# Gate logits from kept transposes: two product blocks a batch instead of four

## The chip, the cores and the metric

The kernel runs on one core of one Trainium2 chip. The metric is the device time of a run in microseconds (us), lower is better. Beside the times of plain runs there is one profiled execution, from which all rows of the trace come.

## The reference

Causal attention over 8 batches, 8 heads, 576 positions and head size 64, with a decay bias from cumulative sums of `s`. Its output, as 4608 tokens of 512 values, goes through a mixture of 8 experts: logits are `x @ w_gate`, tokens are assigned greedily by falling logit with at most 576 tokens an expert, and each expert is a two-layer ReLU network.

```python
scores = scale * np.matmul(q, k.transpose(0, 1, 3, 2))
scores = np.where(causal, -1e9, scores + np.minimum(bias, 0.0))
attn = softmax(scores)                 # maximum taken off, sum + 1e-9
x = np.matmul(attn, v)                 # as N = 4608 tokens x D = 512
logits = x @ w_gate                    # w_gate: 512 x 8
order = np.argsort(-logits.flatten())  # greedy: token and expert once each, 576 tokens an expert
out[mask_e] = np.maximum(x[mask_e] @ w1[e], 0.0) @ w2[e]
```

The change is in the line of the logits.

## The kernel before

**Two parts.** Attention runs first, for 16 groups `g` (a batch `b` = g // 2 and a half `hf` = g % 2 of its heads), each with two passes `pr` of two heads `par`. The experts follow, with a router that picks each expert's tokens.

**Numbers in two pieces.** A value is kept as a hi piece in f16 and a lo piece that holds what f16 left out; a product of two such values takes three matmuls: hi by hi, hi by lo, lo by hi.

**A pass of attention.** `spass` (lines 431 to 501) takes scores on TensorE (PE) into `pss` (three PSUM banks), and VectorE (DVE) takes the row maxima from them at line 442. `sts` (503 to 559) takes the transposed scores into `pst` (three banks, lines 514, 515, 517); ScalarE (ACT) takes exp of them at 525, and GpSimd (POOL) forms the lo piece `R` at 527. `pv` (561 to 592) multiplies with V into `po` (two banks, columns 0 to 324). `norm` (594 to 609) divides by the sums on DVE (lines 602, 603, 604), writes the hi piece of x on ACT (606) and the lo piece on DVE (608) into `xp`. When a batch is done, `xout` stores `xp` into `xs` in DRAM from the SP queue (616, 618).

**The logits.** A pass fills 128 of the 512 columns of x for the 576 tokens of its batch: a quarter `c` = 2 hf + pr. `turn` (621 to 658) transposes that quarter, hi and lo, five token tiles each, on PE (635) into a bank of `pss`, copies it with ACT (638) into `xt` (a ring of three), and multiplies it with the gate `wgp` (645). These products go into columns 340 to 499 of one of the two `po` banks, chosen by the parity of the batch, with one sum for each quarter, token tile and expert. After quarter 3, DVE adds the four quarters (651) into the logits `L`. The router's first steps (lines 797 to 809) run on DVE for batches 0 to 3, 4 to 6 and 7. The expert part begins with `ge` (line 886).

**Order.** Every instruction is a task of `Plan`, a list scheduler with an engine, a duration that the code states, a priority and the buffers that it uses. It plays the schedule through with these stated durations and writes each engine's queue in that order; at run time each queue is served in order. A `Ring` gives out buffers; a ring of one gives the buffer again only when all tasks that use it stand in the plan. The bank of the products isn't among their `uses`. Semaphores are put in by the framework.

Of the kernel before, what the change touches and what calls it, by code (L numbers as in the profile page):

```python
# [10 lines left out]
F16 = mybir.dt.float16  # L11
BF = mybir.dt.bfloat16
I32 = mybir.dt.int32
AF = mybir.ActivationFunctionType
OP = mybir.AluOpType
AX = mybir.AxisListType
# [7 lines left out]
E = 8  # L24
# [180 lines left out]
class Attention:  # L205
# [11 lines left out]
    def rings(self):  # L217
        w, ps = self.w, self.ps
        R = lambda pool, shape, dt, name, n, o=True: Ring([pool.tile(shape, dt, name=f"{name}{i}") for i in range(n)], o)
        self.r = dict(  # L220
            raw=R(w, [128, 2, 2, S], F32, "raw", 2), rv=R(w, [128, 2, 9, D], F32, "rv", 2),
            QK=R(w, [128, 2, 2, 2, HB], F16, "QK", 4),
            V=R(w, [128, 2, 9, 65], F16, "V", 3), Vl=R(w, [128, 2, 9, 64], F16, "Vl", 3),
            P=R(w, [128, 2 * PW + 192], F32, "P", 2), R=R(w, [128, 2 * PW + 192], F16, "R", 2),
            mr=R(w, [128, 10], F32, "mr", 3), ms=R(w, [128, 10], F32, "ms", 2), mp=R(w, [128, 128], F16, "mp", 2),
            mt=R(w, [20, 128], F16, "mt", 2), scr=R(w, [128, 512], BF, "scr", 1, False),
            den=R(w, [128, 5, 2], F32, "den", 3), xp=R(w, [128, 5, 2, DM], F16, "xp", 2),
            xt=R(w, [128, 2, 5, 128], F16, "xt", 3),
            pss=R(ps, [128, 512], F32, "pss", 3, False), pst=R(ps, [128, 512], F32, "pst", 3),
            po=R(ps, [128, 512], F32, "po", 2))  # L230

# [389 lines left out]
    def turn(self, g, pr):  # L621


        nc, pl, k = self.nc, self.pl, self.k
        b, hf = divmod(g, 2)
        c = 2 * hf + pr
        prio = 2 * g + pr + 2.6
        xp, fin = self.xps[b], self.xdone[b][2 * c:2 * c + 2]
        xt, out = self.buf("xt"), []
        for a in range(2):  # L630
            ps = self.buf("pss")

            def turn(a=a, ps=ps):
                for i in range(5):
                    nc.tensor.transpose(ps.t.bitcast(F16)[:, 128 * i:128 * i + 128], xp.t[:, i, a, 128 * c:128 * c + 128],
                                        self.ident16)
            x = pl.add("t", 0.29, turn, [f[a] for f in fin] + [k["i16b"]], prio=prio, uses=[ps, xp])
            out.append(pl.add("a", 0.7, lambda a=a, ps=ps: nc.scalar.activation(
                xt.t[:, a].rearrange("p i c -> p (i c)"), ps.t.bitcast(F16)[:, 0:640], AF.Copy), [x], prio=prio, uses=[ps, xt]))
        o = self.r["po"].slots[b % 2][0][:, 340:500].rearrange("p (k i e) -> p k i e", k=4, i=5)  # L640

        def dots():
            for i in range(5):
                for a, w in ((0, 0), (0, 1), (1, 0)):
                    nc.tensor.matmul(o[:, c, i], xt.t[:, a, i], self.wgp[:, c, w], start=(a, w) == (0, 0), stop=a == 1)
        free = self.lg.get(b - 2, []) if c == 0 else []
        x = self.dots = pl.add("t", 0.44, dots, out + [k["gate"], self.dots] + free, prio=prio + 0.5, uses=[xt])
        if c < 3:
            return
        last = b == self.nb - 1  # L650
        self.lg[b] = ends = [pl.add("v", 0.3, lambda n=n, s=s: nc.vector.tensor_reduce(
            self.L[:n, 5 * b + s.start:5 * b + s.stop], o[:n, :, s].rearrange("p k i e -> p i e k"), AX.X, OP.add),
            [x, k["router"]], prio=prio + 1) for n, s in ((128, slice(0, 4)), (64, slice(4, 5)))]
        self.fresh_lg += ends
        if b in (3, self.nb - 2, self.nb - 1):
            b0 = {3: 0, self.nb - 2: 4}.get(b, b)
            self.router.batch_tasks(pl, b0, b, self.fresh_lg, prio + 2)
            self.fresh_lg = []
# [412 lines left out]
class Moe:  # L1071
# [18 lines left out]
    def expert(self, pl, j, info, behind=None, ident=None):  # L1090
# [10 lines left out]
        for i in range(5):  # L1101
            n = 128 if i < 4 else 64
            g = pl.add("p", 1.25, lambda i=i, n=n: nc.gpsimd.indirect_dma_start(  # L1103
                out=xg.t[:n, i], out_offset=None, in_=self.xs,
                in_offset=bass.IndirectOffsetOnAxis(ap=ids.t[:n, i:i + 1], axis=0)), [ti], prio=1,
                takes=[] if i else [xg], uses=[ids] + ([xg] if i else []), lat=2.2, kb=2 * n)
            tg.append(g)
            tk = dict(takes=[] if i else [xT], uses=[xg] + ([xT] if i else []))
            if ident is None:
                X[i] = pl.add("s", 1.3, lambda i=i, n=n: nc.sync.dma_start_transpose(xT.t[:, i, :, :n], xg.t[:n, i]), [g],  # L1110
                              prio=1, lat=2.6, kb=3.3 * n, **tk)
            else:
                pb = buf("ps")

                def turn(i=i, n=n, pb=pb):
                    ps = pb.t.bitcast(F16).rearrange("p (c t) -> p c t", c=8)
                    for c in range(8):
                        nc.tensor.transpose(ps[:, c, :n], xg.t[:n, i, 128 * c:128 * c + 128], ident[:n, :n])
                t = pl.add("t", 0.5, turn, [g], prio=1, takes=[pb], uses=[xg])
                X[i] = pl.add("a", 1.02 if i < 4 else 0.6, lambda i=i, n=n, pb=pb: nc.scalar.activation(  # L1120
                    xT.t[:, i, :, :n], pb.t.bitcast(F16).rearrange("p (c t) -> p c t", c=8)[:, :, :n], AF.Copy), [t],
                    prio=1, takes=tk["takes"], uses=[pb] + ([xT] if i else []))
# [213 lines left out]
```

## Time and profile before

| what | value |
|---|---|
| median of 3 runs | 827.95 us (824.45 to 829.34) |
| profiled execution, its time | 835.8 us |
| its span from first to last instruction | 834.1 us |
| granted TensorE clock, mean over the span | 0.942 |
| PE busy | 740.5 us, 89% of the span |
| weight loads (PEld) busy | 466.9 us, 56% |
| DVE busy | 605.6 us, 73% |
| ACT busy | 379.8 us, 46% |
| POOL busy | 348.1 us, 42% |

A busy time is summed over the whole span, while attention (to about 350 us) and the experts have different limits, so a stage has to be looked at by itself. A busy PE isn't PE at its peak: matmuls overlap, and their ends are modelled. In rows of the timeline the first number is the start and the second the length in us; `x15` is the number of instructions merged; in brackets stands the idle time before them and what ended it. In groups the numbers behind a colon are least, median and greatest ns of one instruction.

### The profile page before, as it was taken

How to read it: one execution, taken by the hardware profiler on the slowest of the kernel's cores; microseconds unless marked ns; L12 is line 12 of the kernel's file. 1: busy time of each engine (PE TensorE's matmuls, PEld its weight loads, DVE VectorE, ACT ScalarE, POOL GpSimd, SP SyncE). 2: the span in 40 equal slices, each digit the busy share in tenths (PEclk: the TensorE clock that was granted, in tenths of full speed). 3: DMA queues.
4: the chain of work that ended last, by engine and by line, in shares of the span. 5: the costliest groups of instructions: out<-in, count | busy, mean ns of one | idle time of the engine just before them, and what ended most of it. 6: DMA issues, size and time to landing. Idle time of an engine off the chain costs nothing.

```text
span 834.1 us, 23171 instructions
## 1 busy us (share of the span) xinstructions
PE 740.5 (89%) x9059; PEld 466.9 (56%) x9059; DVE 605.6 (73%) x1992; ACT 379.8 (46%) x724; POOL 348.1 (42%) x423
## 2 busy tenths in 40 slices
PE   5288999999989999624999999999999799999995
PEld 1167777877778778512854545545555355454542
DVE  7679999999999997457885786867869568550110
ACT  2366877887768766503441233422334223441210
POOL 5178878878878888302013031121322112401011
PEclk8599999999999999855799999999999999999998
DMA  4955758685657511105238266392735937961001
GB/s 138 288 146 161 229 154 229 191 227 152 195 163 214 145 32 60 58 1 181 80 128 213 72 174 162 127 226 91 187 118 149 193 93 180 262 186 39 20 14 45
DMA packets 85316, 119.30 MB, mean 143 GB/s; under 512 B 40726, under 2 KB 57238, under 8 KB 85206
## 3 DMA queue, kind: packets, MB, share of 16 engines
q1 hardware_dynamic: 79318, 98.93, 43.3%
q0 software_dynamic: 5888, 18.88, 7.9%
q8 instruction: 71, 1.16, 0.6%
q14 instruction: 39, 0.32, 0.1%
HBM read 71.67 MB, written 19.10 MB: 109 GB/s over the span
## 4 chain that ended last, share of the span: by engine, by line
PE 44%; issue 18%; DVE 17%; DMA 5%; POOL 4%; ACT 1%; another core or an unknown queue 0%; SPq 0%; POOLq 0%; DVEq 0%; ACTq 0%
PE psm L1169 13%; PE psm L1243 10%; DVE scr L442 6%; DVE QK L381 3%; PE pst L514 2%; DMA xg<-xs,ids 2%; PE pst L515 2%; PE pss L473 2%; PE psm L1240 2%; PE psn L1173 2%; PE psa L909 2%; PE po L587 2%; POOL out_dram L1223 2%; PE po L589 2%; PE po L588 1%
## 5 line engine op out<-in xcount | busy, mean ns | idle before, releaser
L527 POOL TENSOR_TENSOR R<-P 128x512 f16<-128x512 f32 (+1 forms) x224 | 236.9, 1083 | 45.0 <-ACT P L525 43.9
L1169 PE MATMUL psm<-xT,w1p 128*128 128x512 f16 (+1 forms) x876 | 197.4, 358 | 0.0
L1243 PE MATMUL psm<-w2p,hT 128*128 128x512 f16 x768 | 178.5, 383 | 0.0
L1173 PE MATMUL psn<-xT,w1p 128*128 128x64 f16 x768 | 142.2, 193 | 0.0
L525 ACT ACTIVATE P<-pst 128x512 f32<-128x512 f32 (+1 forms) x224 | 117.6, 548 | 51.4 <-PE pst L517 26.7
L442 DVE CUSTOM_DVE_ANT_0 scr<-pss,mS 128x512 bf16<-128x512 f32 (+3 forms) x256 | 124.1, 485 | 12.2 <-PE pss L473 1.8
L1169 PEld LDWEIGHTS <-w1p 128*128 128x128 f16 x876 | 81.8, 100 | 80.1
L1103 POOL DMA_INDIRECT xg<-xs,ids x40 | 42.2, 1055 | 199.1 <-DVE sg L805 96.3
L1223 POOL DMA_INDIRECT out_dram<-y,ids x40 | 41.6, 1040 | 196.1 <-ACT y L1254 164.4
L1243 PEld LDWEIGHTS <-hT 128*128 128x128 f16 x768 | 70.3, 98 | 81.1 <-issue 5.4
L587 PE MATMUL po<-V,P 128*128 128x65 f16 x960 | 110.1, 195 | 2.3 <-DVE xp L608 1.8
L514 PE MATMUL pst<-QK 70*128 70x64 f16 (+4 forms) x512 | 105.4, 249 | 7.1 <-DMA QK<-mt 6.7
L589 PE MATMUL po<-V,R 128*128 128x65 f16 x960 | 110.2, 193 | 0.1
L588 PE MATMUL po<-Vl,P 128*128 128x64 f16 x960 | 109.9, 192 | 0.0
L515 PE MATMUL pst<-QK 128*128 128x64 f16 (+4 forms) x512 | 104.9, 248 | 0.0
L587 PEld LDWEIGHTS <-P 128*128 128x128 bf16 x960 | 89.6, 97 | 9.3 <-issue 6.7
L588 PEld LDWEIGHTS <-P 128*128 128x128 bf16 x960 | 89.1, 99 | 7.3 <-issue 3.5
L1189 ACT ACTIVATE hT<-psm 128x512 f16<-128x512 f32 x64 | 38.2, 597 | 119.1 <-PE psm L1169 94.8
L473 PE MATMUL pss<-QK 67*128 67x512 f16 (+3 forms) x256 | 72.9, 307 | 20.3 <-DVE mr L442 13.5
L589 PEld LDWEIGHTS <-R 128*128 128x128 f16 x960 | 89.1, 97 | 0.3 <-POOL R L527 0.3
L1173 PEld LDWEIGHTS <-w1p 128*128 128x128 f16 x768 | 72.8, 98 | 0.7
L1254 ACT ACTIVATE y<-psm 128x512 f32<-128x512 f32 x32 | 19.1, 596 | 114.5 <-PE psm L1243 103.6
(202 smaller groups left out, 1396.0 us busy)
## 6 DMA issues: line engine op xcount, KB each, us to landing
QK<-QK SPq DMA_DIRECT2D x120, 144.0 KB
wst<-in_w_dram SPq DMA_DIRECT2D x32, 512.0 KB
wst<-in_w_dram SPq DMA_DIRECT2D x64, 256.0 KB
rv<-in_v_dram SPq DMA_DIRECT2D x16, 576.0 KB
raw<-in_q_dram SPq DMA_DIRECT2D x15, 576.0 KB
raw<-in_k_dram SPq DMA_DIRECT2D x15, 576.0 KB
xs<-xp SPq DMA_DIRECT2D x8, 1024.0 KB
xs<-xp SPq DMA_DIRECT2D x8, 128.0 KB
```

Source lines behind the costliest of these rows:

```text
L442: return pl.add("v", dur, lambda: nc.vector.tensor_tensor_reduce(scr.t[:, :n], ps(), mask, 1.0, init() if init else -3e38, OP.add, OP.max, ...
L473: nc.tensor.matmul(ps.t[:, :n], F()[:, q0:q0 + 128], F()[:, k0:k0 + n], start=True, stop=True)
L514: nc.tensor.matmul(ps[:, c0:c0 + n], F()[:, ks:ks + 128], F()[:, q:q + n], start=True, stop=False)
L515: nc.tensor.matmul(ps[:, c0:c0 + n], G()[:, ks:ks + 128], G()[:, q:q + n], start=False, stop=not diag)
L525: e = pl.add("a", n / 1200 + 0.171, lambda: nc.scalar.activation(P.t[:, c0:c0 + n], ps.t[:, :n], AF.Exp, scale=1.0 / YS), [x] + fresh, pri ...
L527: sub = lambda eng: eng.tensor_tensor(R.t[:, c0:c0 + n], P.t[:, c0:c0 + n], strided_hi(P.t)[:, c0:c0 + n], op=OP.subtract)
L587: nc.tensor.matmul(o[:, i], H[:, c:c + 128], V.t[:, pr, sl], start=f, stop=False)
L588: nc.tensor.matmul(o[:, i, 0:64], H[:, c:c + 128], Vl.t[:, pr, sl], start=False, stop=False)
L589: nc.tensor.matmul(o[:, i], R.t[:, c:c + 128], V.t[:, pr, sl], start=False, stop=l)
L1169: nc.tensor.matmul(ps[:, tiles[0]:tiles[-1] + 1] if len(tiles) > 1 else ps[:, tiles[0]], lhs(f, c, a), xT.t[:, tiles[0]:tiles[-1] + 1, 4 * ...
L1173: nc.tensor.matmul(pt.t[:, 64 * f:64 * f + 64], lhs(f, c, a), xT.t[:, 4, 4 * b + c, 0:64], start=s, stop=e)
L1243: nc.tensor.matmul(py.t, hT.t[:, f, a, 128 * i:128 * i + 128], w2p.t[:, f, b], start=f == 0 and k == 0, stop=f == 7 and k == 2)
```

## The change

- The ring `xt` of three buffers (one quarter each) becomes `xT`, one buffer for all four quarters of a batch. The turns and copies stay as they are, with another place to write to.
- Quarters 0 and 1 issue no products. After quarter 2 the products of quarters 0, 1 and 2 are issued in one task, after quarter 3 those of quarter 3.
- For a token tile and a quarter there are two products instead of three: the hi piece of x with both pieces of the gate side by side (16 columns), and the lo piece of x with the gate's hi piece (8 columns).
- The sums over quarters 0 to 2 and over hi and lo of x are taken in PSUM; four values for each logit (two blocks by two gate pieces) are left for DVE to add, as before four quarters.
- The stated duration is 0.78 us for the first task and 0.26 us for the second; before it was 0.44 us for each of four. The wait for the logits of two batches earlier moves from quarter 0 to quarter 2.

```diff
-            xt=R(w, [128, 2, 5, 128], F16, "xt", 3),
+            xT=R(w, [128, 4, 2, 5, 128], F16, "xT", 1),
...
-        xt, out = self.buf("xt"), []
+        if c == 0:
+            self.xT, self.turned = self.buf("xT"), []
+        xT = self.xT
...
-            out.append(pl.add("a", 0.7, lambda a=a, ps=ps: nc.scalar.activation(
-                xt.t[:, a].rearrange("p i c -> p (i c)"), ps.t.bitcast(F16)[:, 0:640], AF.Copy), [x], prio=prio, uses=[ps, xt]))
-        o = self.r["po"].slots[b % 2][0][:, 340:500].rearrange("p (k i e) -> p k i e", k=4, i=5)
-
-        def dots():
+            self.turned.append(pl.add("a", 0.7, lambda a=a, ps=ps: nc.scalar.activation(
+                xT.t[:, c, a].rearrange("p i c -> p (i c)"), ps.t.bitcast(F16)[:, 0:640], AF.Copy), [x], prio=prio, uses=[ps, xT]))
+        if c < 2:
+            return
+        o = self.r["po"].slots[b % 2][0][:, 340:500].rearrange("p (i k x) -> p i k x", i=5, k=2)
+        cs = range(3) if c == 2 else range(3, 4)
+
+        def dots(h=c - 2):
             for i in range(5):
-                for a, w in ((0, 0), (0, 1), (1, 0)):
-                    nc.tensor.matmul(o[:, c, i], xt.t[:, a, i], self.wgp[:, c, w], start=(a, w) == (0, 0), stop=a == 1)
-        free = self.lg.get(b - 2, []) if c == 0 else []
-        x = self.dots = pl.add("t", 0.44, dots, out + [k["gate"], self.dots] + free, prio=prio + 0.5, uses=[xt])
+                for n in cs:
+                    nc.tensor.matmul(o[:, i, h], xT.t[:, n, 0, i], self.wgp[:, n].rearrange("p w e -> p (w e)"),
+                                     start=n == cs[0], stop=False)
+                    nc.tensor.matmul(o[:, i, h, 0:E], xT.t[:, n, 1, i], self.wgp[:, n, 0], start=False, stop=n == cs[-1])
+        free = self.lg.get(b - 2, []) if c == 2 else []
+        x = self.dots = pl.add("t", 0.26 * len(cs), dots, self.turned + [k["gate"], self.dots] + free, prio=prio + 0.5, uses=[xT])
+        self.turned = []
...
-            self.L[:n, 5 * b + s.start:5 * b + s.stop], o[:n, :, s].rearrange("p k i e -> p i e k"), AX.X, OP.add),
+            self.L[:n, 5 * b + s.start:5 * b + s.stop], o[:n, s].rearrange("p i k (w e) -> p i e (k w)", w=2), AX.X, OP.add),
```

## The prediction

> **What bounds the kernel now.** I read the page first (engines, slices), then the busy times of the stretch that holds the changed code, then the groups of line 645, then who waited for whom, and last the chain that ended last.
>
> ```profile
> span 834.1 us, 23171 instructions
> PE   5288999999989999624999999999999799999995
> DVE  7679999999999997457885786867869568550110
> ...
> 80.00:320.00 240.00, 228.80 (x4382) 185.50 (x4380) 228.04 (x775) 181.13 (x390) 197.28 (x202) 1.00 0.60 170
> ```
>
> The last row lists PE, weight loads, DVE, ACT and POOL, then PE's granted clock. A slice is 834.1/40 = 20.9 us. Attention fills the first 17, up to about 350 us; the experts follow and contain nothing of this change. In the steady stretch PE is busy 228.80 of 240 us and DVE 228.04: 95% each. DVE's instructions stand one behind another, so its 95% is real; PE's are pipelined, so its 95% is an upper figure, and its weight loads cover only 185.50 us (77%). So neither engine alone is the bound; they hand short buffers to each other. The clock is 1.00 throughout and can't improve.
>
> ```profile
> L645 PEld LDWEIGHTS <-xt x480: 94/96/116, 77.2 to 351.1; 128*128 128x128 f16 x160
> L645 PE MATMUL po<-wgp,xt x480: 165/166/189, 77.2 to 351.1; 128*128 128x8 f16 x160
> ...
> 104.90 0.52 PE L645 MATMUL po<-wgp,xt 128*128 128x8 f16 x15
> 143.40 0.52 PE L645 MATMUL po<-wgp,xt 128*128 128x8 f16 x15
> ...
> 344.19 0.03 PE po L587
> 344.22 0.03 PE po L588
> ```
>
> This is the gate's product: 480 in all, 32 blocks (four quarters of each of eight batches) of 15. One matmul lasts 166 ns, but a block only 0.52 us, so one product follows another after (0.52 - 0.166)/14 = 0.0253 us. The nearest wider products with a weight load each, 65 columns, stand 0.03 us apart on the chain.
>
> The next fence has the pieces of the chain of waits (start, length) that are line 645: the blocks that really lay on the path.
>
> ```profile
> 96.68 0.36 PE po L645 x15
> 115.36 0.37 PE po L645 x15
> 124.90 0.36 PE po L645 x15
> 143.56 0.36 PE po L645 x15
> 151.71 0.36 PE po L645 x15
> 188.23 0.37 PE po L645 x15
> 207.14 0.36 PE po L645 x15
> 257.56 0.36 PE po L645 x15
> 285.38 0.36 PE po L645 x15
> 302.83 0.37 PE po L645 x15
> 311.06 0.37 PE po L645 x15
> 319.47 0.37 PE po L645 x15
> 326.79 0.37 PE po L645 x15
> 346.28 0.53 PE po L645 x15
> ```
>
> Fourteen of 32 blocks: thirteen of about 0.37 us in the steady part, one of 0.53 us in the end part. A removed product is therefore worth its time in a little under half of the cases.
>
> **The change part by part.** Products: 3 per token tile and quarter become 2, so 480 become 320. The new hi product has 16 columns instead of 8, a form not in this trace. Its price lies between 0.0253 us (8 columns) and 0.03 us (65 columns); I take 0.0253, since 16 is far nearer to 8. PE work removed: 160 x 0.0253 = 4.0 us; with the other end for the 160 wide products, 160 x 0.0047 = 0.8 us less, so 3.2 us.
>
> What of it lies on the path: by quarter, the four blocks of a batch follow each other about 9 us apart from 77.2 us on, so the thirteen steady pieces are four of quarter 0 (115.36, 151.71, 188.23, 302.83), two of quarter 1 (124.90, 311.06), four of quarter 2 (96.68, 207.14, 285.38, 319.47) and three of quarter 3. Quarters 0 and 1 lose their block, quarter 2 has 30 products instead of 15, quarter 3 has 10. If exactly these stay on the path: 6 x -0.37 + 4 x 15 x 0.0253 - 3 x 5 x 0.0253 = -2.2 + 1.5 - 0.4 = -1.1 us. If which of them is on the path is chance, a third of the thirteen goes: -13 x 0.37/3 = -1.6 us. I take -1.6, because the order changes anyway, and keep -1.1 as the near end.
>
> Waits: DVE's norm shares a PSUM bank with the products (po of the batch's parity) and stands behind them at times.
>
> ```profile
> DVE xp L608 <- PE po L645: 0.5, 2, 0.3
> DVE po L604 <- PE po L645: 0.3, 1, 0.3
> DVE den L602 <- PE po L645: 0.3, 1, 0.3
> ...
> PE pss L473 <- DVE mr L442: 5.6, 13, 0.7
> ```
>
> The columns are us in total, times, longest, between 60 and 320 us. DVE's waits for products are 1.1 us in four; the last row is for a rival below. With 16 blocks instead of 32, half goes, but a block of quarter 2 lasts 29 x 0.0253 + 0.166 = 0.90 us instead of 0.52, so a hit there costs 0.38 us more. Two hits left, one of them longer: -0.55 + 0.38 = -0.2 us. Ends: -1.1 (all gone) and the slower rival below.
>
> The end of attention, from the timeline:
>
> ```profile
> 345.78 0.44 ACT L606 ACTIVATE xp<-po 128x320 f16<-128x320 f32 x1
> 346.90 0.49 DVE L608 TENSOR_TENSOR xp<-po,xp 128x320 f16<-128x320 f32 x1 [0.49 <-PE po L645]
> ...
> 349.52 6.23 DMA xs<-xp
> ...
> 351.32 0.38 DVE L651 TENSOR_REDUCE L<-po 128x32 f32<-128x128 f32 x2 [2.24 <-PE po L645]
> 353.05 0.16 DVE L809 CAST w<-dg 128x5 bf16<-128x5 int32 x1
> 356.17 0.82 DVE L886 TENSOR_TENSOR ge<-w,kj 128x1280 f16<-128x1280 bf16 x1 [2.96 <-DMA xs<-xp]
> ```
>
> The last batch's quarter 2 block (346.28) holds DVE's L608 back by 0.49 us: its input from ACT was there at 346.22. L608 leads over the last norm to the store of xs, and the router's first DVE step waits for that store. With 30 products the block ends 15 x 0.0253 = 0.38 us later: +0.38 us on the path. Quarter 3's block at 350.8 becomes 5 x 0.0253 = 0.13 us shorter, hidden: the logits are done at 353.2, 3 us ahead of the store. If the store came earlier, those 3 us would be the next limit; nothing here comes near.
>
> ACT's copies write the same 640 values, to a bigger tile: 0. L651 reads the same 128 values a partition with another stride: 0, and only the last of its eight pairs lies near the path. No DMA is touched; SP's and POOL's queues are passed by nothing. The products of quarters 0 to 2 now stand on PE's queue behind later scores, P-times-V and turns; nobody but L651 wants them, and that still waits for quarter 3. The new wait is for xT, of which there is one: the first copy of a batch stands behind quarter 3's products of the batch before, and behind it on ACT stand the exps that POOL's R steps need.
>
> ```profile
> 149.71 1.29 ACT L638 ACTIVATE xt<-pss 128x640 f16<-128x640 f16 x2
> ```
>
> For batch 1 to batch 2 the products end at 143.40 + 0.52 = 143.92 and the copy starts at 149.71: 5.8 us of cover, the least of the seven. If it were gone, each us lost would stop ACT and hold one of three pss banks. I cost it at 0.
>
> Sum: -1.6 - 0.2 + 0.4 = -1.4 us. The profiled execution took 835.8 us, 7.85 us above the median of 827.95 of the runs shown; against its own time the forecast is 834.4, against the median 826.5 us.
>
> **One row weighed against the skill.** The stretch shows DVE and PE both at 95%, PE's weight loads at 77%. The Trainium skill, "Perfetto Trace Analysis", section "Identifying the Most-Contended Engine", says that occupancy finds the bottleneck, except on TensorE, where weight-load share is to be used in place of matmul share; by that DVE is the bound and PE's saving would be worth nothing. The trace agrees only partly, since fourteen blocks lie on the path; the rule's outcome is the first rival.
>
> **The rivals.** *DVE alone is the bound.* For it: DVE has 12 us of idle time in 240, and in 60 to 320 us no wait of DVE for a product is longer than 0.3 us. PE's freed time then turns into PE waiting for DVE, which the trace knows already (5.6 us at line 473). Steady part 0, end part +0.4: 828.3 us. Against it: the pieces above.
>
> *PE alone is the bound.* All 4.0 us count, and DVE's waits of 1.1 us go; with the 0.4 of the end, 828.0 - 4.0 - 1.1 + 0.4 = 823.3 us, faster by 0.6%. For it: PE's 228.80 of 240 us, and its slices at digit 9. Against it: DVE's equal share, and that PE itself waits for DVE.
>
> *Slower: the long block holds the bank.* Quarter 2's 30 products sit in the bank which a norm on DVE (L602, L604, L608) and ACT (L606) wants. Hit fully, as at 346.28, a block costs 0.90 us; eight of them 7.2 us, less 1.1 for waits that go and 1.6 for the saving: +4.5, 832.5 us. It decides from the eighth hit in eight for 0.5%, and from three (2.7 us) it eats the gain. Against it: four waits for 26 blocks now, the longest 0.3 us. The products write columns 340 to 499 and the norm reads columns 0 to 324, and still L608 waited 0.49 us for them. The Trainium skill, "PSUM — Partial Sum Buffer", section "PSUM bank collisions raise a hardware error", says that engines must be kept apart by bank, not by address; that wait agrees, and by the rule a longer block makes such waits longer, as this rival has it.
>
> *Another order.* A list scheduler with costs writes every queue; its cost of the products falls from 4 x 0.44 to 0.78 + 0.26 us a batch, and all that follows may fall otherwise. Between like blocks of quarter 0 on the chain, one batch takes 151.71 - 115.36 = 36.35 us, and 188.23 to 302.83 three at 38.2: up to 1.8 us between batches (part of it the router's steps). Eight such draws give 1.8 x 2.8 = 5 us, an estimate from these rows, either way: 821.5 to 831.5 us around the forecast.
>
> **How the numbers follow.** A change within 0.5% (4.1 us) can't be told from none here. Forecast as summed 0.40, DVE alone 0.10: together 0.50 for the same. PE alone 0.18 and a lucky order 0.12: 0.30 faster. Long block 0.07 and an unlucky order 0.13: 0.20 slower. The likeliest is 826.5 us; its own range is 823.3 to 829.3 (from PE alone up to the highest of the three runs of before, 829.34, which lies past DVE alone). The range over the cases: from 819.5 (an order 5 us better on a run 2 us low) to 832.5 (the long block), with 0.2 outside.
>
> **What would show it.** Line 645's successors: 160 matmuls of 128x16 and 160 of 128x8, blocks of 30 (0.90 us or less) and 10 (0.40 us), spaced 0.025 us. PE's busy time between 80 and 320 us falls by about 3 us; if the steps are right, half of it turns into PE waiting for DVE's line 442. L608 before the last norm waits about 0.9 us for the block of 30. The first ge (line 886) starts at 356.17 - 1.4 us. Wrong would be: 16 columns at more than 0.03 us, ACT waiting at line 638 for products, DVE waits for products above 3 us in sum, or the expert stage (from ge to the end, 478 us) differing by more than a us or two, which the change has no hand in.

## The result and the profile after

The changed kernel takes 837.46 us (835.85 to 839.15 in 4 runs) beside 827.37 us (824.45 to 829.34 in 4 runs) for the kernel before: ratio 1.0125 [1.0086, 1.0164]. It is slower by 10 us and outside the forecast range. The profiled execution took 836.49 us. Here and below a ratio and its interval leave out executions in a slow state, such as those over 1.5% above the fastest of their kernel, while a median is of all runs, so a ratio need not be the quotient of two medians.

The page of the kernel after, its span and slices, and PE's and DVE's busy time in the steady stretch (same columns as before):

```profile
span 834.6 us, 22838 instructions
PE   4299698999989999933799999999999999999995
DVE  7669889699898999657787796776968769550110
...
80.00:320.00 240.00, 221.36 (x4065) 178.69 (x4064) 218.00 (x732) 178.12 (x372) 187.23 (x195) 0.96 0.60 170
```

The span is as long as before's (834.1), which misleads. Attention is longer: PE's dip between the two parts, digits 6 2 4 in slices 17 to 19 of before, reads 3 3 7 in slices 18 to 20 of after. From the fourth maxima step on POOL (line 493, at 60.82 us in before; the expectations call it the third) to the issue of the last store of `xs`, attention took 349.52 - 60.82 = 288.7 us before and 360.36 - 62.20 = 298.2 us after. Another execution of the unchanged kernel (below, "again") gave 290.4, so the loss is 7.8 to 9.5 us. The expert part, from the first `ge` to the end, was 477.9 us in the profiled execution of before, and 468.4 in that other one; after has 469.6. The first profile of before was a long one there, and hides the loss.

PE has lost 7.4 busy us in the stretch (228.80 to 221.36), more than the 4.0 us of the 160 products, and DVE, which lost no work, 10.0. Both waited. PE's greatest waits between 60 and 320 us (total us, times, longest), after:

```profile
PE pss L473 <- DVE mr L442: 7.2, 14, 1.4
PE pst L514 <- DMA QK<-mt: 6.7, 3, 3.4
PE pss L495 <- DVE mr L442: 1.8, 3, 1.4
```

The same rows of before:

```profile
PE pss L473 <- DVE mr L442: 5.6, 13, 0.7
PE pss L495 <- POOL mp L493: 2.2, 2, 1.3
PE pss L457 <- DVE mr L442: 2.0, 4, 1.1
...
PE pst L514 <- DMA QK<-mt: 0.4, 1, 0.4
```

The new row is the wait for `mt`: the row maxima, which line 499 sends by a small DMA on SP's queue into the operand of the transposed scores (line 514). The chain of waits of after has that DMA twice at nearly 6 us (start, length):

```profile
97.89 5.78 DMA QK<-mt
...
139.42 5.97 DMA QK<-mt
```

Why it is late stands in SP's timeline of after, around the first of them and the second (start, length of the issue, line):

```profile
96.15 0.39 SPq L616 DMA_DIRECT2D xs<-xp  x1
96.58 0.51 SPq L618 DMA_DIRECT2D xs<-xp  x1
97.89 0.69 SPq L499 DMA_DIRECT2D QK<-mt  x1
...
138.38 0.38 SPq L616 DMA_DIRECT2D xs<-xp  x1
138.82 0.51 SPq L618 DMA_DIRECT2D xs<-xp  x1
139.42 1.28 SPq L499 DMA_DIRECT2D QK<-mt  x1
```

SP's timeline of before, at the first place:

```profile
92.07 0.69 SPq L499 DMA_DIRECT2D QK<-mt  x1
93.37 0.39 SPq L616 DMA_DIRECT2D xs<-xp  x1
93.81 0.50 SPq L618 DMA_DIRECT2D xs<-xp  x1
```

Before issues the 7th of the 32 transfers of maxima, and then the two stores of batch 0 (1024 KB and 128 KB); the 11th and then the stores of batch 1. After has it the other way round in these two batches. It also has the 27th between the two stores of batch 5 and the 31st behind those of batch 6, but there PE doesn't wait. Behind the 1152 KB of batches 0 and 1 the maxima land 5.8 and 6.0 us after their issue. PE's timeline of after shows the price (in brackets the idle time and what ended it):

```profile
103.72 0.38 PE L514 MATMUL pst<-QK 70*128 70x512 f16 x1 [3.36 <-DMA QK<-mt]
...
145.43 0.58 PE L514 MATMUL pst<-QK 70*128 70x512 f16 x1 [2.59 <-DMA QK<-mt]
```

In before the first of these scores started at 98.86 us without a wait. And the idle time isn't all of it: the stretches of 5 us behind these places (PE, weight loads, DVE, ACT, POOL, then the granted clock) read in after

```profile
100.00:105.00 5.00, 1.64 (x24) 1.12 (x21) 1.76 (x8) 1.30 (x5) 1.03 (x3) 0.93 1.01 327
105.00:110.00 5.00, 5.00 (x74) 3.98 (x72) 3.53 (x13) 2.24 (x6) 3.66 (x3) 0.73 0.24 58
...
145.00:150.00 5.00, 4.57 (x44) 3.37 (x44) 3.03 (x9) 1.19 (x2) 2.14 (x3) 0.52 0.53 125
150.00:155.00 5.00, 5.00 (x83) 4.10 (x82) 1.85 (x10) 3.12 (x8) 3.15 (x4) 0.80 0.55 131
```

The granted clock, 1.00 here before, falls to 0.73, and to 0.52 and 0.80: in its busy time PE did 5.00 x 0.27 + 4.57 x 0.48 + 5.00 x 0.20 = 4.5 us less work than at full clock, an estimate from these rows. With the two waits (3.36 + 2.59) that is 10.5 us, enough for the 7.8 to 9.5 that attention lost. The Trainium skill, "TensorE: Matmul & The Clock Gate", section "Part 1: The HAM clock gate", says that an array left idle for about 3.4 us is throttled to half rate. The first wait, 3.36 us, agrees; the second was only 2.59 us, and the clock fell further, to 0.52, so here a shorter idle time was enough.

So the change's own edit isn't what the profile points at. The list scheduler was told other tasks and durations for the products, placed everything anew, and on SP's queue two neighbours changed places. That is an argument so far; the experiments separate the order from the products.

### The profile page after: what moved, and what is told of

It reads as the page before. It is cut to its first block, busy times and chain, and to the rows that moved or that the text cites. A ratio compares the mean times of both kernels' runs of the same rounds, so it can differ in the third digit from the quotient of the medians.

```text
span 834.6 us, 22838 instructions
## 1 busy us (share of the span) xinstructions
PE 737.2 (88%) x8899; PEld 465.4 (56%) x8899; DVE 606.6 (73%) x1992; ACT 382.7 (46%) x724; POOL 344.8 (41%) x423
## 4 chain that ended last, share of the span: by engine, by line
PE 54%; issue 15%; DVE 14%; DMA 9%; POOL 4%; ACT 1%; another core or an unknown queue 1%; SPq 1%; POOLq 0%; DVEq 0%; ACTq 0%
PE psm L1177 15%; PE psm L1251 10%; DVE scr L442 4%; PE pst L514 4%; PE pst L515 3%; DMA QK<-mt 3%; PE pss L473 3%; PE po L587 2%; PE po L589 2%; POOL R L527 2%; PE po L588 2%; PE psm L1248 2%; PE psn L1181 2%; DMA raw<-in_k_dram 2%; PE psa L917 2%
## 5 line engine op out<-in xcount | busy, mean ns | idle before, releaser
L527 POOL TENSOR_TENSOR R<-P 128x512 f16<-128x512 f32 (+1 forms) x224 | 231.4, 1059 | 44.6 <-ACT P L525 44.2
L1177 PE MATMUL psm<-xT,w1p 128*128 128x512 f16 (+1 forms) x876 | 195.1, 353 | 0.0
L1251 PE MATMUL psm<-w2p,hT 128*128 128x512 f16 x768 | 175.3, 379 | 0.0
L1177 PEld LDWEIGHTS <-w1p 128*128 128x128 f16 x876 | 79.6, 98 | 80.4 <-issue 0.3
L514 PE MATMUL pst<-QK 70*128 70x64 f16 (+4 forms) x512 | 108.2, 254 | 13.8 <-DMA QK<-mt 12.9
L587 PE MATMUL po<-V,P 128*128 128x65 f16 x960 | 112.8, 197 | 1.9 <-DVE xp L608 1.2
L589 PE MATMUL po<-V,R 128*128 128x65 f16 x960 | 112.8, 195 | 0.5 <-POOL R L527 0.5
L588 PE MATMUL po<-Vl,P 128*128 128x64 f16 x960 | 112.5, 194 | 0.0
L515 PE MATMUL pst<-QK 128*128 128x64 f16 (+4 forms) x512 | 108.1, 254 | 0.0
L587 PEld LDWEIGHTS <-P 128*128 128x128 bf16 x960 | 91.5, 99 | 10.0 <-issue 6.4
L588 PEld LDWEIGHTS <-P 128*128 128x128 bf16 x960 | 90.9, 100 | 8.2 <-issue 3.8
L1181 PEld LDWEIGHTS <-w1p 128*128 128x128 f16 x768 | 72.7, 98 | 0.7
```

Of the source, the lines that this page charges most:

```text
L514: nc.tensor.matmul(ps[:, c0:c0 + n], F()[:, ks:ks + 128], F()[:, q:q + n], start=True, stop=False)
L515: nc.tensor.matmul(ps[:, c0:c0 + n], G()[:, ks:ks + 128], G()[:, q:q + n], start=False, stop=not diag)
L527: sub = lambda eng: eng.tensor_tensor(R.t[:, c0:c0 + n], P.t[:, c0:c0 + n], strided_hi(P.t)[:, c0:c0 + n], op=OP.subtract)
L587: nc.tensor.matmul(o[:, i], H[:, c:c + 128], V.t[:, pr, sl], start=f, stop=False)
L588: nc.tensor.matmul(o[:, i, 0:64], H[:, c:c + 128], Vl.t[:, pr, sl], start=False, stop=False)
L589: nc.tensor.matmul(o[:, i], R.t[:, c:c + 128], V.t[:, pr, sl], start=False, stop=l)
```

## The experiments

The kernel before ran beside each set, with a median of 829.17 us (*new products, old order*; *old products, new order*; *store behind the maxima*; *maxima behind the store*), 824.05 (the three on what the products are worth, and *before, told 0.26*), 828.77 (*only the small store ahead*, *even blocks of 20 in that order*, *each store but the last*, *before once more*), 829.85 (the three under *can the planner be told*) and 823.82 (the last three). Each ratio is to the kernel before of the same set. "Attention" is the length defined above, from one profile each; two profiles of the kernel before differ in it by 1.7 us (288.7 and 290.4). Lines behind 442 stand one to six lower in some of these kernels (L516 for L514).

**Order or products?** *New products, old order.* The plan is told the old four tasks of 0.44 us and gives each engine the old order; what is issued is the new products.

```diff
-            xT=R(w, [128, 4, 2, 5, 128], F16, "xT", 1),
+            xt=Ring(["", "", ""], True),     # for the plan alone; xT is one tile beside it
...
-        cs = range(3) if c == 2 else range(3, 4)
+        cs = {2: range(3), 3: range(3, 4)}.get(c, [])
...
-        x = self.dots = pl.add("t", 0.26 * len(cs), dots, self.turned + ...
+        x = self.dots = pl.add("t", 0.44, dots, out + ...
```

> The changed kernel's products (blocks of 30 and 10, 16 columns, kept xT), but the planner is told the old tasks, so that every queue is in the order of the kernel before. Theory Q (the store of xs stands ahead of the maxima's small DMA on SP's queue in batches 0 and 1, and PE waits for that DMA and loses its clock): nothing of the slowdown is left, the products give their 1 to 2 us: 825 to 827.5 us, ratio 0.997 to 1.000. Theory O (the order as a whole, many small waits): the same here. Theory P (the long block, the bank or the one xT costs the time): 834 to 838 us, ratio 1.008 to 1.0125.

Measured: 833.38 us, 1.0053 [1.0028, 1.0078]; attention 291.2.

*Old products, new order.* After, with three products of 8 columns for each tile and quarter (480 again, in blocks of 45 and 15), told the same durations as after.

```diff
-                    nc.tensor.matmul(o[:, i, h], xT.t[:, n, 0, i], self.wgp[:, n].rearrange("p w e -> p (w e)"), ...
+                    nc.tensor.matmul(o[:, i, h, 0:E], xT.t[:, n, 0, i], self.wgp[:, n, 0], ...
+                    nc.tensor.matmul(o[:, i, h, E:], xT.t[:, n, 0, i], self.wgp[:, n, 1], ...
```

> The changed kernel's order on every queue, but three products of 8 columns for each pair instead of two (480 in all, blocks of 45 and 15). Theories Q and O: all of the slowdown stays, and the 160 products more cost up to 4 us on PE: 837 to 841 us, ratio 1.012 to 1.017. Theory P: longer blocks are worse still where the long block is the cause, 841 us or more; if the 16-column form is the cause, 827 to 830 us.

Measured: 836.8 us, 1.0099 [1.0065, 1.0134]; attention 298.3, as long as after's 298.2, and the waits for the maxima's DMA are as long in sum (6.7 in after):

```profile
PE pst L514 <- DMA QK<-mt: 7.2, 5, 2.5
```

With the old number of products the loss is there, so it is the order's. That the 160 products make no difference to attention here holds within the 1.7 us between profiles. The old order with the new products keeps a smaller loss, which is taken up below.

**Is it the store ahead of the maxima?** *After, store behind the maxima.* Only in batches 0 and 1, both stores are written behind the next maxima; all else in after's order.

```diff
+        def put():                       # the maxima's task
+            nc.sync.dma_start(QK.t[67:69, 0, 0, pr], mt.t)
+            while self.held:
+                self.held.pop(0)()
...
+        late = lambda f: (lambda: self.held.append(f)) if b < 2 else f      # the tasks of both stores
```

> The changed kernel with one swap on SP's queue in each of batches 0 and 1: the two DMAs of the store of xs are written behind the maxima's DMA that followed them. All else on every queue is as in the changed kernel. Theory Q: PE's waits for QK<-mt at 100 and 143 us (3.4 and 2.6 us) and the half clock after them go, some 4 to 5 us each: 827 to 830 us, ratio 1.000 to 1.003. Theory O: one spot of many, 833 to 836 us. Theory P: no change, 837 us.

Measured: 829.36 us, 1.000 [0.997, 1.0031]; attention 290.0. The neighbours put back in two batches, and the slowdown is gone. The wait rows of this kernel, and its steady stretch:

```profile
PE pss L473 <- DVE mr L442: 8.3, 18, 1.4
PE pss L495 <- DVE mr L442: 1.8, 3, 1.4
PE pss L643 <- DVE mr L442: 1.6, 5, 0.8
...
PE pst L516 <- DMA QK<-mt: 0.4, 1, 0.4
...
80.00:320.00 240.00, 226.14 (x4219) 182.92 (x4218) 225.96 (x757) 183.06 (x383) 194.87 (x203) 0.99 0.59 169
```

The wait for the maxima is at 0.4 us, as before. These rows also show what the saving is worth once nothing disturbs it: PE is 2.7 us less busy than before (228.80), and its waits for DVE's maxima grow from 8.4 us (5.6 + 2.0 + 0.5 + 0.3; 9.5 in the second profile of before) to 11.7.

*Before, maxima behind the store.* The reverse in before, for the same two batches.

```diff
+            f = lambda: nc.sync.dma_start(QK.t[67:69, 0, 0, pr], mt.t)
+            self.held.append(f) if n0 in (6, 10) else f()     # held until the second store is issued
```

> The kernel before with the opposite swap: in batches 0 and 1 the maxima's DMA is written behind the two DMAs of the store of xs. Theory Q: PE waits some 3 us for QK<-mt twice and its clock falls: 833 to 838 us, ratio 1.006 to 1.012. Theories O and P: 827 to 830 us, ratio 1.000 to 1.003.

Measured: 826.94 us, 0.9976 [0.9946, 1.0005]; attention 288.3. No loss: a miss for the plain form of the theory. PE's timeline of this kernel:

```profile
97.92 0.38 PE L516 MATMUL pst<-QK 70*128 70x512 f16 x1 [0.17 <-DMA QK<-mt]
```

The maxima were issued at 93.17 us, wanted at 97.75, 4.6 us later, and landed 4.7 us after their issue (in this kernel's chain of waits); in after they were issued at 97.89, wanted at 103.72 - 3.36 = 100.36, 2.5 us later, and landed after 5.8. So the swap alone costs nothing; it costs the landing time less the slack, and the new order had the swap, less slack and a longer landing. Why the same 1152 KB held them 1.1 us longer there is open.

*After, only the small store ahead.* 128 KB ahead of the maxima, 1024 KB behind them: a store still stands in front, with a ninth of the bytes.

```diff
+ batches 0 and 1: store of 128 KB in its place, store of 1024 KB after the next maxima
```

> The changed kernel; in batches 0 and 1 the small DMA of the store (128 KB) stays ahead of the maxima's on SP's queue and the big one (1024 KB) is written behind it. The maxima's DMA is then still issued only when the norm is done, as in the changed kernel, but with a ninth of the bytes ahead of it. Theory Qb (the bytes ahead make it land late, 5.8 and 6.0 us after its issue instead of about 3): PE's two waits for QK<-mt fall from 3.4 and 2.6 us to under 1, and attention ends within 2 us of e5 (last store of xs at 351 to 354 us in the profile), time about as e5, ratio 0.999 to 1.004. Theory Qi (it is issued too late, because SP waits for the norm ahead of it): the waits stay at 2 us or more, last store at 358 to 361 us, ratio 1.008 to 1.012.

Measured: 829.14 us, 1.0001 [0.9973, 1.0028]; attention 289.7. Its wait row:

```profile
PE pst L516 <- DMA QK<-mt: 1.3, 2, 0.8
```

Both of these waits stand elsewhere, at 70.69 and 273.06 us, behind no store; at the two places PE doesn't wait. So it is the bytes ahead, and not the place behind a store as such. The Trainium skill, "DMA: Bandwidth & Descriptors", section "Queues, rings and completion order", says that descriptors are consumed in ring order on each DMA engine; this run, with 128 KB ahead instead of 1152 and no wait, agrees.

**What are the products worth by themselves?** These three keep before's order.

*No products in quarters 0 and 1* (240 of 480 left out; the logits lack two quarters):

```diff
-            for i in range(5):
+            for i in range(5 if c > 1 else 0):
```

> The kernel before with the products of quarters 0 and 1 left out of the computation (the logits are then sums over two quarters). This prices the saving alone. If a third to a half of blocks is on the path: 6 pieces of 0.37 and half of DVE's waits, 2 to 3 us faster, ratio 0.996 to 0.998. If DVE alone is the bound: 0 to 0.5 us, ratio 0.999 to 1.001.

Measured: 821.58 us, 0.9983 [0.9953, 1.0012]; attention 289.0. Half of all products gone, 6 us of PE by the prediction's spacing, and no gain that shows: the ratio lies between the two expectations, and its interval holds both. Its rows:

```profile
PE pss L473 <- DVE mr L442: 8.6, 21, 0.9
PE pss L457 <- DVE mr L442: 2.8, 4, 1.5
...
80.00:320.00 240.00, 226.33 (x4170) 181.66 (x4169) 229.24 (x774) 181.77 (x389) 196.71 (x203) 0.99 0.60 170
```

PE's waits for the maxima are 8.6 + 2.8 and 1.1 in smaller rows, 12.5 us, against 8.4 and 9.5 in the two profiles of before, and DVE is as busy as before (229.24 against 228.04). So the rows, more than the time, say that DVE sets the pace in this order.

*Quarter 2's block doubled* (its 15 products issued twice):

```diff
-            for i in range(5):
+            for i in [*range(5)] * (2 if c == 2 else 1):
```

> The kernel before with quarter 2's 15 products issued twice in a row (30, of 8 columns; the second pass writes the same sums again). This prices the long block alone. Theory L: 8 x 0.38 us at most plus a longer hold of DVE in the end part: 2 to 4 us, ratio 1.002 to 1.005. Rival F: PE has room, 0 to 1 us, ratio 0.999 to 1.001.

Measured: 823.17 us, 0.9984 [0.9959, 1.0009]; attention 292.0. The time is unmoved, and the expected loss of 2 to 4 us isn't there. The lag behind before, from block to block on PE, grows in steps of 0.3 to 0.4 us at four of the eight blocks; attention is between 1.6 and 3.3 us longer.

*Even blocks of 20* (10 fewer products a half batch, issued after quarters 1 and 3), old order:

```diff
-        cs = {2: range(3), 3: range(3, 4)}.get(c, [])
+        cs = {1: range(2), 3: range(2, 4)}.get(c, [])
```

> As e1 (two products for each pair, order of the kernel before), but the blocks are even: 20 products after quarter 1 (quarters 0 and 1) and 20 after quarter 3 (quarters 2 and 3). Theory L (what e1 lost, 0.5%, is the block of 30 that holds back DVE's norm in the same PSUM bank): the long block is gone, four of 32 blocks a pair of batches less, 825 to 828 us against 829.2, ratio 0.995 to 0.999. Rival F (the 16-column form, or sums kept open in PSUM, cost the time, however the blocks are cut): as e1, 832 to 834 us, ratio 1.004 to 1.006.

Measured: 823.0 us, 0.997 [0.9938, 1.0002]; attention 288.9. All the saving and no long block: no loss, as expected, and no gain that can be told from none. So of the 1.0053 of the first experiment, the cut into 30 and 10 is the likely part: the products are as many here, only cut otherwise. How it would cost that isn't shown. A long block that holds back DVE's norm does stand in DVE's timeline of that first kernel (new products, old order), but once:

```profile
136.57 0.17 DVE L604 TENSOR_SCALAR den<-po 128x5 f32<-128x5 f32 x1 [0.16 <-PE po L650]
```

That 0.16 us is all that DVE waits for products there between 60 and 320 us, and the doubled block lost no time. Its attention, 291.2, is 0.9 to 2.5 us above before's, while its time is 4.2 us above; the cause isn't settled.

**Does any stated duration move the time?** *Before, told 0.26 instead of 0.44.* Nothing on the chip changes but the order.

```diff
-        x = self.dots = pl.add("t", 0.44, dots, ...
+        x = self.dots = pl.add("t", 0.26, dots, ...
```

> The kernel before with one number changed, the stated duration of a block of products (0.26 instead of 0.44 us); every instruction is the same, only the planner's order differs. SP's queue then has the store of xs ahead of the maxima in batch 0 alone. Theory Q (a store ahead costs where the maxima are issued less than about 5 us before PE wants them): between 828 and 835 us, ratio 1.000 to 1.006, with a wait of PE for QK<-mt in the trace if it is above 1.002. Theory O (any new order is about as good): 826 to 832 us, no such wait.

Measured: 820.05 us, 0.9934 [0.9902, 0.9967]; attention 289.8. A gain, below what either theory expected, though the store does stand ahead of the maxima in batch 0 (PE waits 0.44 us for them there). It isn't in attention, and the profile doesn't show where else: that execution took 825.17 us, and its expert part 464.4 against 461 to 463 in the three others of its set. Left open.

*Even blocks of 20 in that order:*

```diff
+ blocks of 20 as above, told 0.26 for each of four tasks
```

> e7's products (two for each pair, blocks of 20) in the order of e3 (stated duration 0.26 us). If e3's 0.7% and e7's 0.3% are both real and add: ratio 0.988 to 0.993. If e3's gain isn't in attention (its profile has attention 1 us longer than before) but a chance of the expert stage: ratio 0.994 to 1.001.

Measured: 828.28 us, 0.997 [0.9938, 1.0002]; attention 288.2. The gain of 0.66% isn't seen again with another content in that order.

*After with even blocks, each store but the last behind the next maxima* (planned anew):

```diff
-        cs = range(3) if c == 2 else range(3, 4)
+        cs = range(c - 1, c + 1)       # after quarters 1 and 3
+ stores of batches 0 to 6 issued right after the next maxima
```

> The changed kernel with even blocks of 20 (after quarters 1 and 3), which gives the planner another order again, and every store of xs but the last written behind the next maxima. If late maxima and the long block are what the change lost: no wait of PE for QK<-mt above 1 us after 60 us, attention as long as in e7 (289 us from the third mp step to the last store) or up to 2 us longer, ratio 0.995 to 1.001. If a new order loses some 5 us whatever stands on SP's queue: ratio 1.003 to 1.01.

Measured: 832.05 us, 1.0042 [1.0014, 1.0069]; attention 292.6. A miss: the second outcome came. It is another order again, and in it PE waits for the maxima 3.3 us in three places, none behind a store:

```profile
PE pst L516 <- DMA QK<-mt: 3.3, 3, 2.1
```

*The kernel before once more*, as a control for these sizes:

> The kernel before, unchanged, as a control: how far two sets of runs of the same program differ, and how long its expert stage (from the first ge to the end) is on this chip beside those of the others. Ratio 0.998 to 1.002; expert stage within 4 us of the other profiles of this call.

Measured: 827.72 us, 0.9983 [0.9959, 1.0007]; attention 290.4, expert part 468.4. So between two profiles of one program attention differs by 1.7 us and the expert part by 9.5.

**Can the planner be told?** The plan gives the maxima's DMA a fixed 2.3 us to land. A task with `kb` also waits, in the plan, for the bytes issued earlier (at 270 KB/us). So the maxima's task gets a small `kb`:

```diff
-            uses=[mt, QK], lat=2.3)
+            uses=[mt, QK], lat=2.3, kb=5)
```

*After with it:*

> The changed kernel; the planner is told that the maxima's DMA goes through the same shared transfer as the others (kb=5 in its task), so that behind a store it lands 4 us later in the plan; before, the plan gives it 2.3 us after its issue whatever is ahead. Theory B (the change lost its time since the plan was blind to that): no wait of PE for QK<-mt above 1 us after 60 us, attention from the third mp step to the last store 288 to 292 us, ratio 0.997 to 1.003. Theory O (a new order loses some us by chance wherever): ratio 1.003 to 1.012.

Measured: 821.96 us, 0.9896 [0.9861, 0.993]; attention 282.9. Faster than either theory expected; PE waits nowhere for the maxima's DMA.

*After with it and even blocks of 20:*

> As e13 with even blocks of 20 after quarters 1 and 3. Theory B: attention 287 to 291 us, ratio 0.995 to 1.001. Theory O: 1.002 to 1.01.

Measured: 818.65 us, 0.9857 [0.9801, 0.9914]; attention 280.9. Again faster than expected.

*Before with it:*

> The kernel before with the same one number for the planner. Its order had no such wait, so by theory B nothing is to be won: attention 288 to 291 us, ratio 0.997 to 1.003. Theory O: anything from 0.993 to 1.01.

Measured: 809.04 us, 0.9756 [0.972, 0.9793]; attention 337.24 - 59.60 = 277.6. The expectation that there was nothing to win in before is refuted: one number in the plan, and not one instruction more or less, wins 20.8 us, 11 to 13 of them in attention. Another 1.2 to 2.8 come ahead of it: the fourth maxima step starts at 59.60 us instead of 60.82 or 62.36. Its rows:

```profile
PE pss L473 <- DVE mr L442: 0.7, 1, 0.7
...
80.00:320.00 240.00, 237.63 (x4650) 195.36 (x4648) 222.12 (x784) 190.94 (x406) 195.16 (x215) 1.00 0.60 166
```

PE is now busy for 237.63 of 240 us. The waits for DVE's maxima, 8.4 us before, are nearly gone, and DVE has 18 us to spare. That looks as if PE alone were the bound, which the next experiments try. Part of DVE's room comes from its own instructions, which are the same but shorter in this order. Line 381, which forms lo pieces of q and k, stands so in DVE's groups between 60 and 340 us (count | busy us, mean ns), before and here:

```profile
L381 DVE SCALAR_TENSOR_TENSOR QK<-raw,QK 128x1152 f16<-128x1152 f32 x26 | 43.1, 1687 | 0.0
...
L381 DVE SCALAR_TENSOR_TENSOR QK<-raw,QK 128x1152 f16<-128x1152 f32 x24 | 34.1, 1425 | 0.0
```

That is 24 x 0.262 = 6.3 us less of DVE's time. In the same way POOL's 224 steps of line 527 fall from a mean of 1083 ns to 1028. Whether this causes the gain or goes with it wasn't tried, and which of the moved places does it isn't settled; before had only 0.4 us of waits for the maxima's DMA in this stretch, so it isn't those waits themselves.

**And the change in that order?** PE busy for 99% is the case in which a saving on PE should count. All three have the order of the last kernel.

*Blocks of 20:*

```diff
+ products in blocks of 20 after quarters 1 and 3; the plan told four tasks of 0.44 us, and kb=5
```

> e15's order on every queue (the old tasks, the maxima's DMA with kb=5), with the new products in even blocks of 20. In e15 PE is busy 99% between 80 and 320 us. Theory S (the saving was worth nothing in the old order since DVE, at 95%, and the hand-overs set the pace; where PE is full it counts): 2 to 4 us below e15, attention 274 to 276 us from the third mp step to the last store (e15: 277.6). Rival N (the saving is worth nothing in any order): as e15 within 1 us.

Measured: 806.45 us, 0.98 [0.9765, 0.9835]; attention 276.7.

*Blocks of 30 and 10, as in the change:*

```diff
+ products in blocks of 30 and 10 after quarters 2 and 3; the plan told four tasks of 0.44 us, and kb=5
```

> e15's order with the changed kernel's own products (blocks of 30 and 10). Theory S: 1 to 4 us below e15; theory L (the block of 30 holds DVE): 1 to 2 us above e16. Rival N: as e15 or up to 2 us slower.

Measured: 810.82 us, 0.9837 [0.9801, 0.9874]; attention 280.4.

*Before with `kb=5` once more:*

> e15 unchanged on the chip of this call, for the comparison with e16 and e17: ratio to the kernel before 0.972 to 0.980, attention within 1 us of 277.6.

Measured: 805.26 us, 0.9779 [0.9747, 0.981]; attention 277.6. So the gain repeats. The saving of 160 products, 4.0 us of PE, goes with an attention 0.9 us shorter and no gain in time (0.98 against 0.9779); that it would count in full here is refuted, so a PE that the profile shows busy for 99% isn't shown to be the bound. The change's own blocks are slower than the old products here: 810.82 against 805.26 us in six runs each, side by side, with attention 2.8 us longer in one profile each. No version is shown to be faster than the kernel before with that one number, 2.2 to 2.4% faster than before.

## Why the prediction was wrong

**The step that failed is "No DMA is touched; SP's and POOL's queues are passed by nothing."** The edit moves no DMA, but the plan moved SP's stores past the maxima in batches 0 and 1, since it was told other tasks and durations. That step was the whole result, within the interval: with the two pairs put back the ratio is 1.000 [0.997, 1.0031]. The product tasks alone were followed through the queues, and not the queues themselves.

**"Another order" was the rival that came true, and mis-sized.** It was put at 5 us either way, from like blocks of one trace. Such rows show how an order varies within itself; they can't show a transfer that gets another one in front of it. The orders tried here gave from 277.6 us of attention (before with `kb=5`) to 298.3 (old products, new order): 21 us with the same products. A sign stood in the trace of before, outside the stretch from 60 us on that was searched for waits; its timeline:

```profile
39.79 0.58 PE L514 MATMUL pst<-QK 70*128 70x512 f16 x1 [6.33 <-DMA QK<-mt]
```

The same small DMA already had PE waiting for 6.3 us at the start of attention; before with `kb=5` has no such wait.

**"I take -1.6" for the products on the path isn't borne out.** The times alone leave room for it: with 240 products left out the interval of the ratio runs from 3.9 us faster to 1.0 slower. But attention doesn't move beyond the 1.7 us between profiles, neither for 160 products (new order) nor for 240 (old order). That a block lies on the chain of waits doesn't mean that the end moves when it goes; PE then waits longer for DVE (12.5 us instead of 8.4 and 9.5). In this the rows side with the rival "DVE alone is the bound", and with it with the rule from the Trainium skill, "Perfetto Trace Analysis", section "Identifying the Most-Contended Engine", which was given a chance of 0.10. They do so in the order of before; with `kb=5` DVE is idle for 18 us of 240, with the same instructions. So the prediction's "its 95% is real" needs a limit: 6.3 us of that busy time (line 381, above) went away in another order.

**The long block.** "+0.38 us on the path" at the end was right: L608 of the last norm waits for products, as DVE's timeline of after shows, where 0.49 stood before:

```profile
357.73 0.49 DVE L608 TENSOR_TENSOR xp<-po,xp 128x320 f16<-128x320 f32 x1 [0.86 <-PE po L652]
```

In the steady part the long block was put at a chance of 0.07 for a loss of 4.5 us. The block doubled by itself lags by 0.3 to 0.4 us at half of its places and can't be seen in the time; the change's own blocks cost 0.5% in before's order, and with `kb=5` the ratio is 0.9837 with them against 0.98 with blocks of 20 and 0.9779 with the old products (neighbouring intervals overlap). So the cut into 30 and 10 was the worse one in both orders, as this rival has it, but its mechanism isn't shown: DVE hardly waits for products in those kernels (0.2 and 0.6 us between 60 and 320 us).

**What held.** The prices of the products, from the groups of after:

```profile
L650 PE MATMUL po<-wgp,xT x160: 169/169/193, 99.2 to 361.6; 128*128 128x16 f16 x160
...
L652 PE MATMUL po<-wgp,xT x160: 166/166/190, 99.3 to 361.6; 128*128 128x8 f16 x160
```

16 columns last 3 ns longer than 8, and both follow each other after 0.025 us. DVE waits for products only 0.4 us in sum between 60 and 320 us, and ACT never waits for the products before it fills `xT`: the cover that was costed at nothing was there. The fall of PE's busy time by about 3 us was right once the stores are put back (2.7), but all of it turned into waiting for DVE, and not half. The first `ge` came at 365.00 us, 8.8 later than in before and not 1.4 earlier. Of the signs of being wrong one came, and it says nothing of the change: the expert part differs by 8.3 us, and by 9.5 between two profiles of the kernel before.

## What to carry to other kernels

Where a planner writes the queues, an edit that changes a task or its stated duration can be a new order of every queue: compare the order of each queue before and after, the DMA queue first, and price each small transfer that comes to stand behind a large one by its landing time less the time until it is wanted. Search for such waits over the whole span, start included. And a change's own worth is seen only with the order held fixed; here no gain showed, while one number that tells the plan about the bytes ahead was worth 2.2 to 2.4%, for reasons that are open in part.

## What was not expected of the hardware

A small DMA issued right behind 1152 KB on the same queue landed after 5.8 and 6.0 us in after, and after 4.7 us in before with the maxima behind the store; in after's chain others with no store right ahead took 3.0 to 4.9 us. With 128 KB ahead PE didn't wait for it. Idle times of PE of 3.4 and 2.6 us were followed by granted clocks of 0.73 and of 0.52 in the next stretches, so each such wait cost more than itself. After has a third such fall, to 0.76 and 0.56 between 245 and 255 us, where PE doesn't wait for this DMA, and the kernel with the store behind the maxima has one too (0.51 and 0.81 between 240 and 250 us); what sets it off is open. And the expert part, whose instructions no experiment changed, took from 461 to 478 us from profile to profile; what sets it wasn't tried.
